# Rebalancing a scheduled attention and gated-FFN kernel: fewer operations on GpSimd, P also scaled by ScalarE

## The chip, the cores and the metric

The kernel runs on one core of one Trainium2 chip. The core has a matrix engine (TensorE, PE in the profile), three engines for elementwise work (VectorE or DVE, ScalarE or ACT, GpSimd or POOL), and SyncE (SP), which here issues nearly all transfers. Each engine runs its own list of instructions in order and waits on semaphores for the others. The metric is the device time in microseconds, the median over runs.

## The reference

Attention over q, k, v of shape (8 batches, 8 heads, 576 positions, 64), followed by a normalised gated feed-forward over the 4608 resulting rows of 512.

```python
scores = q @ k.T / 8
mask_local   = (rel >= 0) & (rel < 32)                    # heads 0..3, rel = i - j
mask_strided = (rel >= 0) & (j % 32 == i % 32)            # heads 4..7
attn = softmax(where(mask, scores, -1e9)) @ v
x  = attn.transpose(0, 2, 1, 3).reshape(4608, 512)
xn = x / sqrt(mean(x * x) + 1e-6) * rms_g
y  = (silu(xn @ w_gate) * (xn @ w_val)) @ w_out           # 512 -> 1536 -> 512
```

## The kernel before, in words

The rows of x are cut into nine chunks of 512, one per 512 columns of a matmul. The feed-forward is the dense work: weights and activations are split into a high and a low part (xh, xl, hh, hl), and three products of 128x512 matmuls stand for one in full precision. Chunks 0 to 2 go unit by unit (12 units of 128 hidden columns): L1040 makes g and v, L1053 and L1055 turn g into a gate, L1066 multiplies by v (one "gate" per unit, 36 in all), L1073 and L1082 split the product, L1092 multiplies by w_out. Chunks 3 and 4, then 5 and 6, then 7 and 8 go in pairs with a seven-product scheme (L1851 for two of the pairs, L1464 and L1630 for the last). During chunk 0 the weights are converted as they arrive (L2072 to L2094), and once during the first half transforms of the weights are made (L1144, L1148, L1230 to L1241).

The attention of later batches is woven between these dense matmuls. Its unit is a batch, two heads and up to two tiles of queries. Two units make a pair, and pairs alternate between two buffers, pp0/pT0 and pp1/pT1. A pair goes: scores on PE into one PSUM bank (L614; earlier units L715), row maxima and the masked copy out of the bank on DVE (L620), exponentials on ACT (L627), row sums and their reciprocals on DVE (L642, L643, tile my), normalising P by them on POOL (L650, tile pp, one instruction per unit), a transpose on DVE (L664), and seven block moves pp to pT that SP issues (L667). Two pairs are a group; its values are made on PE together (L836, into the same bank) and copied to raw, the rows of x, by ACT (L881) or DVE (L883). Then come squares and roots of a chunk (L916, L921, L980 to L990).

The order of all this is not written out. `Plan.op` collects operations with a cost in ns, what they read and write, and the engines that may run them. `forward` is a list scheduler: for each engine it takes the operations that can start soonest (within a "hold", one number per engine) and among them the one with the earliest due time; of an operation with two possible engines it takes an engine only if no other would finish it sooner. `port` marks operations which the plan lets run on only one of VectorE and GpSimd at a time. `series` and `latest` work out due times in rounds, with the sets PASS_A and PASS_B (holds; spacing of chains; allowance for a transfer; rounds). The resulting order of each engine is fixed in the program.

Of the kernel before, what the change touches and what calls it, by code (L numbers as in the profile page):

```python
# [14 lines left out]
AF = mybir.ActivationFunctionType  # L15
# [17 lines left out]
NX = 3  # L33
# [5 lines left out]
RES0 = [0, 7, 14, 20, 26]  # L39
NEG = -1.0e9  # L40
NCST = 512
DW = 4
VIN = 4
MSL = 8
# [50 lines left out]
MARG = 0.0  # L95
# [36 lines left out]
PVF = 1  # L132
HLO = 9
TABLE = 1283.0
PORT = True
PASS_A = ([0.0, 0.0, 150.0, 400.0], 0.4, 4000.0, 7)
PASS_B = ([25.0, 450.0, 300.0, 800.0], 0.1, 8000.0, 9)
SWITCH = 220000.0
PLAP = 140.0
LATE = -100000.0  # L140
# [21 lines left out]
class Plan:  # L162
# [18 lines left out]
    def op(self, eng, cost, at, fn, reads=(), writes=(), bytes_=0, rel=0.0, lock=(), tab=None, port=False, chain=False, also=None, early=0.0):  # L181
        i = len(self.ops)
        self.early.append(early)
        self.lift.append(0.0 if chain else self.boost)
        deps = set()
        for r in reads:
            if r in self.writer:
                deps.add(self.writer[r])
        for w in writes:
            if w in self.writer:  # L190
                deps.add(self.writer[w])
            deps.update(self.readers.get(w, ()))
        for r in reads:
            self.readers.setdefault(r, []).append(i)
        for w in writes:
            self.writer[w] = i
            self.readers[w] = []
        deps.discard(i)
        if eng == "PE":
            if self.serial:  # L200
                deps.add(self.last_pe)
            self.last_pe = i
        if also is None:
            ways = {eng: (cost, port or eng == "Pool", fn)}
        else:
            ways = {e: (c, p or e == "Pool", lambda e=e: fn(e)) for e, c, p in [(eng, cost, port)] + list(also)}
        self.ops.append((ways, deps, bytes_, rel, lock, tab, chain))
# [64 lines left out]
    def forward(self, users, due, hold, due2=None, hold2=None):  # L272
        ops, n = self.ops, len(self.ops)
        left = [len(o[1]) for o in ops]
        end, on = [0.0] * n, [None] * n
        ready = [None] * n
        free, avail = {}, {}

        def enter(i):
            ways, deps, _, rel, _, _, _ = ops[i]  # L280
            ready[i] = {e: max([end[d] + (0.0 if on[d] == e and not ops[d][2] else self.lat(i)) for d in deps] + [rel]) for e in ways}
            for e in ways:
                avail[e].append(i)
        for o in ops:
            for e in o[0]:
                free.setdefault(e, 0.0)
                avail.setdefault(e, [])
        for i in range(n):
            if not left[i]:
                enter(i)  # L290
        dma = 0.0
        held = {}
        table = "exp"
        port = (0.0, None)
        names = ("PE", "DVE", "ACT", "Pool")
        out = []

        def start(i, e):
            s = max(free[e], ready[i][e])
            for b in ops[i][4]:  # L300
                t, who = held.get(b, (0.0, e))
                s = max(s, t if who == e else t + self.LAT)
            if ops[i][0][e][1] and port[1] != e:
                s = max(s, port[0])
            return s
        while len(out) < n:
            best = None
            for e, lst in avail.items():
                cand = []
                for i in lst:  # L310
                    s = start(i, e)
                    ways = ops[i][0]
                    if len(ways) > 1:
                        f = s + ways[e][0] - MARG
                        if any(x != e and start(i, x) + ways[x][0] < f for x in ways):
                            continue
                    cand.append((s, due[i] - self.lift[i], i))
                if not cand:
                    continue
                soon = min(cand)[0] + (hold[names.index(e)] if e in names else 0.0)  # L320
                k = min((c for c in cand if c[0] <= soon), key=lambda c: (c[1], c[0], c[2]))
                if best is None or k < best[0]:
                    best = (k, e)
            (s, _, i), e = best
            ways, _, nb, _, lock, tab, _ = ops[i]
            cost, pt, fn = ways[e]
            if tab and tab != table:
                table = tab
                cost += TABLE
            done = s + cost + self.TAIL[e]  # L330
            for b in lock:
                held[b] = (done, e)
            if pt:

                port = (done - PLAP, e)
            for x in ways:
                avail[x].remove(i)
            free[e] = s + cost
            on[i] = e
            if nb:  # L340
                dma = max(dma, s) + nb / 380.0
                end[i] = dma + 2000.0
            else:
                end[i] = done
            out.append((i, e, s, end[i]))
            if due2 is not None and s > SWITCH:
                due, hold = due2, hold2
            for u in users[i]:
                left[u] -= 1
                if not left[u]:  # L350
                    enter(u)
        return out
# [3 lines left out]
def attn_moe(ctx: ExitStack, tc: tile.TileContext, qT: bass.AP, kT: bass.AP, vl: bass.AP, vs: bass.AP,  # L356
             wgv: bass.AP, wo: bass.AP, gain: bass.AP, consts: bass.AP, out: bass.AP):
    nc = tc.nc
# [68 lines left out]
    def dve(n, rate=0.96):  # L427
        return 75 + n / rate
# [4 lines left out]
    def way(name, *ways):  # L433

        return [w for w in ways] if name in ALT else []
# [162 lines left out]
    def step_e(i):  # L598
# [31 lines left out]
        def rest():  # L630
# [14 lines left out]
            for y, (m_, n_) in enumerate(((m0, n0), (m1, n1))):  # L645
                def norm(e, y=y, m_=m_, n_=n_):
                    g = slice(4 * y, 4 * y + 4, 3 - n_)
                    s = mx2[x][:m_, y].rearrange("q h t -> q (h t)") if n_ == 2 else mx2[x][:m_, y, :, 0]
                    v = PX[x][:m_, :, g]
                    (nc.vector if e == "DVE" else nc.gpsimd).tensor_tensor(  # L650
                        out=v, in0=v, in1=s.unsqueeze(1).unsqueeze(3).broadcast_to([m_, 4, 2 * n_, 32]), op=ALU.mult)
                op("Pool", 500 * n_, 0, norm, reads=[("sm", x, y)], writes=[("pu", x, y)], also=way("h", ("DVE", dve(256 * n_), True)))
        return scores, rd, 2 * nt * (0.84 * P + 2), rest

    units = []
# [268 lines left out]
    def rms(c, bk, at):  # L924
# [60 lines left out]
        for kc in range(KC):  # L985
            op("DVE", dve(CH) + 50, at + kc,
               lambda kc=kc: nc.vector.scalar_tensor_tensor(out=rt[:, kc], in0=rt[:, kc], scalar=gt[:, kc:kc + 1],
                                                            in1=roots["srt"], op0=ALU.mult, op1=ALU.mult),
               reads=["srt", "gt"], writes=[("raw", c % NX, kc)])

    def convert(c, at, kcs=range(KC)):
        rt = raw[c % NX]
# [1295 lines left out]
```

## Time and profile before

| | |
|---|---|
| runs shown | median 1011.04 us, 1009.02 to 1013.16 |
| the profiled execution: its time | 1004.59 us |
| its span, mean granted clock | 1002.4 us, 0.991 |
| PE / DVE / ACT / POOL busy | 970.6 / 739.5 / 495.9 / 311.9 us |
| DMA, mean over the span | 218 GB/s |

The numbers of the page belong to the one profiled execution, whose time lies 6.45 us below the median of the runs. A busy engine is one whose instructions run; PE's matmuls overlap, so a chain of 128x512 matmuls shows one new start every 0.227 us although one lasts about 0.4. A wait is an engine's idle time with the name of what ended it.

### The profile page before, as it was taken

What the parts mean: (1) busy time and instruction counts of PE and PEld (TensorE: products, weight loads), DVE (VectorE), ACT (ScalarE), POOL (GpSimd) and SP (SyncE); (2) the same over time, 40 slices, a digit from 0 to 9 for tenths busy, and PEclk for the clock granted to TensorE, in tenths of its full rate; (3) what the DMA queues carried; (4) which work ended last, traced back from release to release, by engine and by line L of the source; (5) the groups of instructions that cost most, each with busy time, mean ns of one, the idle gap of its engine ahead of it and who ended that gap; (6) DMA issues with size and microseconds to landing.
All of it is one profiled execution on the core that took longest, in us unless ns stands there. A gap on an engine that the chain in (4) does not pass through costs nothing.

```text
span 1002.4 us, 16255 instructions
## 1 busy us (share of the span) xinstructions
PE 970.6 (97%) x5212; PEld 778.7 (78%) x5212; DVE 739.5 (74%) x1741; ACT 495.9 (49%) x1392; POOL 311.9 (31%) x294
## 2 busy tenths in 40 slices
PE   8899999999998999999999999999999999999998
PEld 6777766778876777887888887888887787888886
DVE  5889999888977859489665648954565888456981
ACT  6999865555456434455555333534252423234530
POOL 6333346776557536135101113110002210001200
PEclk9999999999999999999999999999999999999999
DMA  9999654666656464254766698575587644793551
GB/s 312 367 389 341 222 206 150 219 223 210 221 176 233 144 232 144 63 171 149 237 211 239 213 315 304 181 269 177 171 300 278 209 167 168 238 334 120 159 168 74
DMA packets 88469, 218.13 MB, mean 218 GB/s; under 512 B 11840, under 2 KB 35392, under 8 KB 88384
## 3 DMA queue, kind: packets, MB, share of 16 engines
q1 hardware_dynamic: 87616, 216.23, 62.3%
q10 hardware_dynamic: 768, 0.85, 0.3%
q8 instruction: 42, 0.69, 0.3%
q14 instruction: 43, 0.35, 0.1%
HBM read 162.06 MB, written 47.19 MB: 209 GB/s over the span
## 4 chain that ended last, share of the span: by engine, by line
PE 78%; DVE 8%; DMA 7%; issue 3%; SPq 2%; ACT 2%; POOL 1%; ACTq 0%; DVEq 0%; POOLq 0%
PE acc L1092 18%; PE acc L1851 9%; PE g L1040 8%; PE v L1040 7%; PE g L1851 6%; PE v L1851 6%; PE v L1464 3%; PE pair L1464 3%; PE g L1464 3%; PE pair L614 3%; PE pair L836 2%; PE v L1630 2%; PE g L1630 2%; PE acc L1630 2%; SPq L667 2%
## 5 line engine op out<-in xcount | busy, mean ns | idle before, releaser
L1092 PE MATMUL acc<-or,hh 128*128 128x512 f32 x480 | 153.4, 401 | 0.6 <-POOL or L2094 0.6
L650 POOL TENSOR_TENSOR pp<-pp,my 96x512 f32<-96x512 f32 (+2 forms) x68 | 69.8, 1046 | 231.4 <-DVE my L643 48.3
L627 ACT ACTIVATE pp<-pp,my 96x128 f32<-96x128 f32 (+2 forms) x248 | 96.2, 391 | 39.7 <-DVE my L620 27.8
L1092 PEld LDWEIGHTS acc<-or,hh 128*128 128x128 f32 x480 | 90.3, 191 | 22.3 <-POOL or L2094 1.5
L1040 PE MATMUL g<-xh,wg 128*128 128x512 f32 x288 | 93.0, 404 | 3.0 <-DVE e L1055 3.0
L1092 PE MATMUL acc<-or,hl 128*128 128x512 f32 x240 | 94.7, 395 | 0.6 <-POOL hl L1082 0.6
L1040 PE MATMUL v<-xh,wv 128*128 128x512 f32 x280 | 90.0, 402 | 1.9 <-DVE e L1066 1.2
L1082 POOL TENSOR_TENSOR hl<-e,hh 128x512 fp32r<-128x512 f32 x36 | 52.4, 1455 | 82.3 <-ACT hh L1073 82.2
L620 DVE CUSTOM_DVE_ANT_0 pp<-pair,cb 96x128 f32<-96x128 f32 (+2 forms) x248 | 55.4, 282 | 18.5 <-DMA pT<-pp 8.4
L1040 PEld LDWEIGHTS g<-xh,wg 128*128 128x128 f32 x288 | 51.9, 189 | 16.4 <-DVE e L1055 3.9
L1040 PEld LDWEIGHTS v<-xh,wv 128*128 128x128 f32 x280 | 51.3, 190 | 15.7 <-DVE e L1066 2.5
L1092 PE MATMUL acc<-or,xh 128*128 128x512 f32 x192 | 59.7, 392 | 0.0
L1040 PE MATMUL g<-xl,wg 128*128 128x512 f32 x144 | 56.5, 392 | 0.0
L1040 PE MATMUL v<-xl,wv 128*128 128x512 f32 x140 | 54.8, 392 | 0.0
L1092 PEld LDWEIGHTS acc<-or,hl 128*128 128x128 f32 x240 | 45.8, 191 | 11.1 <-POOL hl L1082 1.1
L627 ACT ACTIVATION_READ_ACCUMULATOR pp<-pp,my 96x1 f32 (+2 forms) x248 | 46.7, 188 | 0.0
L881 ACT COPY raw<-pair 128x192 f32<-128x192 f32 (+12 forms) x103 | 22.9, 348 | 47.4 <-PE pair L836 43.7
L664 DVE STREAM_TRANSPOSE pp<-pp 128x1024 f32<-128x1024 f32 x34 | 42.0, 1237 | 3.2 <-POOL pp L650 3.2
L614 PEld LDWEIGHTS pair<-xx,xx 64*96 64x96 f32 (+2 forms) x496 | 29.2, 170 | 16.7 <-issue 8.5
L1092 PEld LDWEIGHTS acc<-or,xh 128*128 128x128 f32 x192 | 35.7, 188 | 8.1 <-issue 0.5
L614 PE MATMUL pair<-xx,xx 64*96 64x128 f32 (+2 forms) x496 | 36.4, 285 | 4.4 <-ACT raw L881 2.4
L921 POOL TENSOR_TENSOR ssq<-ssq,srt 128x512 f32<-128x512 f32 x21 | 28.7, 1366 | 32.7 <-ACT srt L916 32.7
(661 smaller groups left out, 2496.9 us busy)
## 6 DMA issues: line engine op xcount, KB each, us to landing
or<-wos SPq DMA_DIRECT2D x72, 512.0 KB, 4.4
wv<-wsv SPq DMA_DIRECT2D x29, 512.0 KB, 7.6
or<-tg SPq DMA_DIRECT2D x22, 512.0 KB, 5.8
th<-tg SPq DMA_DIRECT2D x21, 512.0 KB, 6.4
tl<-tg SPq DMA_DIRECT2D x21, 512.0 KB, 4.1
wg<-wsg SPq DMA_DIRECT2D x19, 512.0 KB, 8.7
xx<-in_qT_dram SPq DMA_DIRECT2D x31, 288.0 KB, 5.1
xx<-in_kT_dram SPq DMA_DIRECT2D x28, 288.0 KB, 3.0
```

What stands on the lines that cost most here:

```text
L614: nc.tensor.matmul(out=sp[h][:, t].rearrange("q x k -> q (x k)"), lhsT=qt[r, q0:q0 + m], rhs=kt[r, k0:k0 + P], start=True, stop=True)
L620: nc.vector.tensor_tensor_reduce(out=PX[x][:m, :, g0 + 2 * h + t], in0=sp[h][:, t], in1=mk[t], scale=-0.125, scalar=3.0e38, op0=ALU.add, o ...
L627: nc.scalar.activation(out=v, in_=v, func=AF.Exp, scale=-1.0, bias=mx2[x][:m, u, h, t:t + 1], accum_out=su2_[x][:m, u, h, t, 0:1])
L650: (nc.vector if e == "DVE" else nc.gpsimd).tensor_tensor(out=v, in0=v, in1=s.unsqueeze(1).unsqueeze(3).broadcast_to([m_, 4, 2 * n_, 32]), ...
L664: op("DVE", DVT + 2 * CH / 0.96, 0, lambda: nc.vector.transpose(out=pq[x], in_=pq[x]), reads=[], writes=[("pu", x, 0), ("pu", x, 1), ("pp" ...
L921: op("Pool", pool(CH), at, lambda e: (nc.vector if e == "DVE" else nc.gpsimd).tensor_tensor(out=ssq, in0=ssq, in1=roots["srt"], op=ALU.add ...
L1040: nc.tensor.matmul(out=out, lhsT=wt[:, w, sl], rhs=xhl[x, kc], start=(kc == 0 and i == 0), stop=(kc == KC - 1 and i == 2))
L1082: (nc.vector if n == "DVE" or h else nc.gpsimd).tensor_tensor(out=hl[h], in0=e, in1=hh[h].bitcast(F32), op=ALU.subtract)
L1092: nc.tensor.matmul(out=acc[t], lhsT=x[h][:, sl], rhs=wt[:, w], start=(u == 0 and i == 0), stop=(u == NU - 1 and i == 2))
L1464: nc.tensor.matmul(out=banks[bk], lhsT=w, rhs=X[a, k].tile(y), start=start and k == 0 and i == 0, stop=stop and k == 1 and i == 2, skip_gr ...
L1630: nc.tensor.matmul(out=banks[bks[j]], lhsT=tile(v, k, j), rhs=x.tile(y), start=start and k == 0 and i == 0, stop=stop and k == KT - 1 and ...
L1851: nc.tensor.matmul(out=banks[bk], lhsT=w, rhs=xtile(a, k, y), start=start and k == 0 and i == 0, stop=stop and k == 1 and i == 2, skip_gro ...
```

## The change

Five things change in the plan's rules, and one in the work.

- `POOLP = 700`: where an operation may run on several engines, GpSimd's finishing time counts as 700 ns later.
- The normalising of P for later units (L650) may run on GpSimd or ScalarE; ScalarE then issues one activation (copy with a per-row factor) per head and tile, 4 or 2 per unit. It could run on GpSimd alone before, since `way("h", ...)` is switched off.
- The final scaling of x in `rms` (L987) is marked with `port`, so that the plan keeps it off GpSimd's time. The instruction is the same.
- PE operations outside the dense chains count 80 ns less (`SMD`); among PE operations those of the kind just run are preferred by 600 ns (`KIN`); the cost of a switch of kind is a parameter, zero (`SWC`).
- Transfers are planned at 345 bytes per ns in place of 380 (`DMR`), and the holds and rounds of the two passes are other numbers.

```diff
+POOLP = 700.0
+DMR = 345.0
+SWC = 0.0
+SMD = 80.0
+KIN = 600.0
-PASS_A = ([0.0, 0.0, 150.0, 400.0], 0.4, 4000.0, 7)
-PASS_B = ([25.0, 450.0, 300.0, 800.0], 0.1, 8000.0, 9)
+PASS_A = ([0.0, 0.0, 210.0, 560.0], 0.3, 4000.0, 7)
+PASS_B = ([60.0, 466.0, 445.0, 585.0], 0.1, 4000.0, 11)
...
         if eng == "PE":
+            if not chain:
+                cost = max(cost - SMD, 150.0)
...
-                        f = s + ways[e][0] - MARG
-                        if any(x != e and start(i, x) + ways[x][0] < f for x in ways):
+                        f = s + ways[e][0] - MARG + POOLP * (e == "Pool")
+                        if any(x != e and start(i, x) + ways[x][0] + POOLP * (x == "Pool") < f for x in ways):
                             continue
-                    cand.append((s, due[i] - self.lift[i], i))
+                    cand.append((s, due[i] - self.lift[i] - (KIN if e == "PE" and ops[i][6] == kind else 0.0), i))
...
+            if e == "PE" and ops[i][6] != kind:
+                kind = not kind
+                cost += SWC
...
-                dma = max(dma, s) + nb / 380.0
+                dma = max(dma, s) + nb / DMR
...
+                    if e == "ACT":
+                        for h in range(2):
+                            for t in range(n_):
+                                w = PX[x][:m_, :, 4 * y + 2 * h + t]
+                                nc.scalar.activation(out=w, in_=w, func=AF.Copy, scale=mx2[x][:m_, y, h, t:t + 1])
+                        return
...
-                op("Pool", 500 * n_, 0, norm, reads=[("sm", x, y)], writes=[("pu", x, y)], also=way("h", ("DVE", dve(256 * n_), True)))
+                op("Pool", 500 * n_, 0, norm, reads=[("sm", x, y)], writes=[("pu", x, y)], also=[("ACT", 2 * n_ * 293, False)])
...
-               reads=["srt", "gt"], writes=[("raw", c % NX, kc)])
+               reads=["srt", "gt"], writes=[("raw", c % NX, kc)], port=PORT)
```

Every engine's order differs. Three places follow; line numbers of the change are 11 to 17 higher than those of before.

TensorE, at the end of chunk 2 (units 0 and 1 of the next weights), where the bank "pair" is passed between scores and values. Before, from a group's values on:

```order
L836 MATMUL pair<-pT_98,vt_86 64x128 x2
L836 MATMUL pair<-pT_98,vt_87 64x128 x4
L836 MATMUL pair<-pT_99,vt_87 64x128 x6
L1040 MATMUL v<-xh_676,wv_545 128x512 x2
L1040 MATMUL v<-xl_683,wv_545 128x512
L614 MATMUL pair<-xx_84,xx_83 96x128 x8
```

and in the change, from the scores ahead of the same values on:

```order
L625 MATMUL pair<-xx_84,xx_83 96x128 x4
L1057 MATMUL g<-xh_654,wg_534 128x512 x2
L1057 MATMUL g<-xl_665,wg_534 128x512
L1057 MATMUL v<-xh_654,wv_586 128x512 x2
L1057 MATMUL v<-xl_665,wv_586 128x512
L853 MATMUL pair<-pT_98,vt_86 64x128 x2
L853 MATMUL pair<-pT_98,vt_87 64x128 x4
L853 MATMUL pair<-pT_99,vt_87 64x128 x6
L625 MATMUL pair<-xx_84,xx_83 96x128 x8
```

The next scores follow the values at once (3 dense matmuls stood between), and 6 dense matmuls stand ahead of the values, where 15 did.

GpSimd in chunk 2, two consecutive pairs' P (tiles pp_96 and pp_97). Before:

```order
L650 TENSOR_TENSOR pp_96<-pp_96,my_105 126x4x128
L650 TENSOR_TENSOR pp_96<-pp_96,my_105 108x4x2x32
L1148 TENSOR_TENSOR tt<-tt 128x256
L650 TENSOR_TENSOR pp_97<-pp_97,my_106 108x4x128
L650 TENSOR_TENSOR pp_97<-pp_97,my_106 108x4x2x32
```

and ScalarE in the change, around the end of that chunk (L638 are the exponentials, L898 the copies to raw, L665 the new activations):

```order
L638 ACTIVATE pp_97,sv_107<-pp_97,my_106 96x4x32 x4
L665 ACTIVATE pp_96<-pp_96,my_105 96x4x32 x4
L898 COPY raw_78<-pair 128x6x10
L898 COPY raw_79<-pair 128x6x8
L638 ACTIVATE pp_97,sv_107<-pp_97,my_106 96x4x32 x4
L933 ACTIVATE srt<-raw_78 128x512
```

Of a pair's two units one has gone to ScalarE, between the exponentials of the other buffer.

SyncE, the last two groups of block moves. Before:

```order
L667 DMA pT_98<-pp_96 32x256 x7
L1118 DMA out_dram<-xh_7085 128x512
L1248 DMA tl_7117<-tg_150 128x1024
L1118 DMA out_dram<-xl_7093 128x512
L1248 DMA th_7126<-tg_150 128x1024
L2125 DMA or_7129<-wos_119 128x1024
L667 DMA pT_99<-pp_97 32x256 x7
```

and in the change:

```order
L684 DMA pT_98<-pp_96 32x256 x7
L1265 DMA tl_7085<-tg_150 128x1024
L1265 DMA th_7090<-tg_150 128x1024
L2142 DMA or_7093<-wos_114 128x1024
L2142 DMA or_7114<-wos_115 128x1024
L2142 DMA or_7145<-wos_116 128x1024
L2142 DMA or_7171<-wos_117 128x1024
L1135 DMA out_dram<-xh_7181 128x512
L1135 DMA out_dram<-xl_7187 128x512
L2142 DMA or_7199<-wos_118 128x1024
L684 DMA pT_99<-pp_97 32x256 x7
```

Nine transfers lie between the two groups, where five did, and the two outputs nearest the end of the queue follow the last group instead of preceding it.

More of the change, by code (lines that the diff above doesn't have):

```diff
@@ L294, in forward @@
         port = (0.0, None)
+        kind = False
         names = ("PE", "DVE", "ACT", "Pool")
```

## The prediction

> **What bounds the kernel now.** I read the head of the page first, then the busy time by stretch, then who made TensorE (PE) wait, then the chain of work.
>
> ```profile
> span 1002.4 us, 16255 instructions
> PE 970.6 (97%) x5212; PEld 778.7 (78%) x5212; DVE 739.5 (74%) x1741; ACT 495.9 (49%) x1392; POOL 311.9 (31%) x294
> PE 78%; DVE 8%; DMA 7%; issue 3%; SPq 2%; ACT 2%; POOL 1%; ACTq 0%; DVEq 0%; POOLq 0%
> ```
>
> TensorE is busy for 97% and carries 78% of the chain. The change adds and drops no matrix work, so it can only win or lose where the matmuls wait: 1002.4 - 970.6 = 31.8 us idle, some of it at the two ends, plus what a lowered clock costs. These are the longer waits between the ends (line engine, releaser: total, times, longest):
>
> ```profile
> PE pair L836 <- DMA pT<-pp: 3.7, 2, 2.3
> PE g L1040 <- DVE e L1055: 3.0, 2, 2.0
> PE pair L614 <- ACT raw L881: 2.4, 1, 2.4
> PE pair L715 <- DVE mx L732: 2.3, 1, 2.3
> PE pair L614 <- DVE my L620: 1.8, 2, 1.1
> PE pair L836 <- DVE my L620: 1.5, 1, 1.5
> PE v L1040 <- DVE e L1066: 1.2, 1, 1.2
> PE g L1851 <- DVE or L1901: 1.2, 1, 1.2
> ```
>
> They sum to 17.1 us. Nearly all belong to the attention that is woven between the dense matmuls: scores (L614, L715) wait for the one score bank to be emptied, values (L836) for the probabilities to arrive. No line names POOL, but POOL sits inside those loops. The busy time by stretch shows who is short there (columns: stretch, length, busy PE, PEld, DVE, ACT, POOL, granted clock, DMA share, GB/s):
>
> ```profile
> 100.00:150.00 50.00, 47.73 (x300) 36.00 (x298) 47.07 (x142) 36.40 (x112) 20.77 (x20) 1.00 0.61 217
> 150.00:200.00 50.00, 46.89 (x254) 35.55 (x255) 45.52 (x132) 29.18 (x91) 35.65 (x30) 0.97 0.51 184
> 300.00:350.00 50.00, 44.34 (x287) 34.57 (x286) 39.88 (x121) 30.21 (x102) 31.89 (x29) 0.97 0.58 188
> ...
> 145.00:155.00 10.00, 7.42 (x44) 5.10 (x43) 9.83 (x41) 9.18 (x27) 4.73 (x4) 0.84 0.45 154
> 295.00:310.00 15.00, 12.01 (x84) 9.36 (x85) 12.09 (x48) 10.09 (x40) 8.43 (x9) 0.89 0.72 246
> 355.00:370.00 15.00, 13.00 (x58) 10.17 (x54) 10.38 (x20) 4.48 (x10) 6.22 (x6) 0.89 0.66 210
> 795.00:805.00 10.00, 7.69 (x40) 6.07 (x40) 7.13 (x10) 3.95 (x8) 1.47 (x1) 0.83 0.75 272
> ```
>
> From 100 to 200 us VectorE is 93% busy: that stage is short of VectorE. From 300 to 350 no engine is full and PE stands 5.7 us: that stage is short of time in a loop of hand-offs. And each of the four longest waits is followed by a dip of the granted clock: 10 us at 0.83 instead of 1.00 is 1.7 us lost, and 15 us at 0.89 is 1.65 us. So a wait of two to three microseconds costs about 1.7 us more than itself.
>
> By the Trainium skill ("TensorE: Matmul & The Clock Gate", Part 1) the clock halves after at least one idle window of about 3.4 us. The rows contradict that as a floor: the longest wait listed is 2.4 us and the clock still dipped. By the rule my sum below would lose one 1.7 us term and read -5.4 us.
>
> **The change, part by part.**
>
> *P on two engines.* Normalising P is one instruction per unit on POOL; a pair of units was two in a row, ahead of the transpose. Counted in the order, 35 of 68 go to ScalarE, mostly one unit of each pair; each becomes 2 or 4 small activations (130 in all).
>
> ```profile
> 315.78 2.49 POOL pp L650 x2
> ...
> 318.30 1.25 DVE pp L664
> ...
> 330.78 2.73 PE acc L1092 x12
> ```
>
> ```profile
> L650 POOL TENSOR_TENSOR pp<-pp,my 96x512 f32<-96x512 f32 x32 | 34.5, 1097 | 83.1 <-DVE my L643 31.9 <-DMA xx<-in_kT_dram 24.6 <-DMA pT<-pp 14.2
> L627 ACT ACTIVATE pp<-pp,my 96x128 f32<-96x128 f32 x128 | 49.7, 391 | 17.1 <-DVE my L620 11.6 <-DMA tg<-tl 4.5 <-DMA vt<-in_vl_dram 1.0
> L881 ACT COPY raw<-pair 128x192 f32<-128x192 f32 x29 | 9.2, 356 | 12.8 <-PE pair L836 10.8 <-PE pair L842 2.0
> ```
>
> The new activation has no row. The nearest are the exponential over the same 128 columns with a per-row operand (0.391 us) and a plain copy of 192 (0.356). I take 0.36, nearer the copy, since the new one has a per-row factor but no exponential. Bounds: 0.28 (the copy scaled down from 192 columns, an estimate) to 0.39. Four take 1.4 us beside 1.1 us on POOL, so the pair's two steps last about 1.4 instead of 2.2 to 2.5: roughly 0.9 us less per turnaround. ScalarE gains 130 x 0.36 = 47 us and gives up 18 output copies, 18 x 0.356 = 6.4: +40 on 496, about 54% of the span. In 300 to 350 it stands at 30.2 of 50, which covers the 8 us or so it gets there; without that cover its copies out of the bank (L881) would be late, and with them the next scores.
>
> In the crunch of 295 to 330 us four pairs chase each other through two buffers, two turnarounds in series on each: 2 x 0.9 = -1.8 us. Against it, the new order is tighter there: between the scores of one pair and the following values stand 6 dense matmuls where 15 stood, and behind those values none where 3 stood (three take 0.7 us: the last row of the chain is 12 in 2.73). I charge the 0.7 for the latter, and for the former a quarter of the 2.0 us of lost cover, 0.5, since those values did not wait at all before. Shorter turnarounds also let the evacuation go to whichever of VectorE and ScalarE is free; the wait on ACT L881 (2.4) should halve, -1.2. Term: **-1.8**, bounds -7 (all waits there and the dip) to +4 (tighter order, full price).
>
> *Two late rounds.* Here the order gives more room.
>
> ```profile
> 607.44 0.88 PE L836 MATMUL pair<-pT,vt 108*64 108x128 f32 x12 [1.38 <-DMA pT<-pp]
> ...
> 800.69 1.55 PE L836 MATMUL pair<-pT,vt 128*64 128x96 f32 x16 [2.31 <-DMA pT<-pp]
> ```
>
> ```profile
> 785.27 4.31 SPq L667 DMA_DIRECT2D pT<-pp  x7
> 789.68 0.53 SPq L1118 DMA_DIRECT2D out_dram<-xh  x1
> 790.31 0.38 SPq L1248 DMA_DIRECT2D tl<-tg  x1
> 790.78 0.40 SPq L1118 DMA_DIRECT2D out_dram<-xl  x1
> 791.28 0.38 SPq L1248 DMA_DIRECT2D th<-tg  x1
> 791.75 0.45 SPq L2125 DMA_DIRECT2D or<-wos  x1
> 792.30 5.08 SPq L667 DMA_DIRECT2D pT<-pp  x7
> ```
>
> At 607 the values come 63 dense matmuls after the last scores of their group; in the new order 150. At 0.227 us each that is 20 us more room for a wait of 1.38: it goes, **-1.4** (bounds -1.4 to 0, should the or and w loads ahead on SP's queue still be late). At 800 the room grows from 75 to 84 matmuls, +2.0 us, and the half-turn above gives 0.9; and between the last two groups of seven transfers SP issued five others from 789.68 to 792.30, with 15 dense matmuls between the two scores; the new order has nine there, but 66 matmuls (15 us) to issue them in. 2.9 us covers the 2.31, so the wait goes, and with it the dip of 1.7: **-4.0** (bounds -4.0 to 0, if an output transfer in front holds SP up).
>
> *Bias away from POOL.* 71 instructions leave POOL; 35 are P, the rest go to VectorE, among them all eight weight subtractions L2094; with them come 18 output copies L883.
>
> ```profile
> L2094 DVE TENSOR_TENSOR or<-th,or x8: 678/681/1779, 49.4 to 130.1; 128x512 fp32r<-128x512 f32 x8
> L2094 POOL TENSOR_TENSOR or<-th,or x4: 1260/1278/1751, 58.0 to 175.6; 128x512 fp32r<-128x512 f32 x4
> ...
> L883 DVE COPY raw<-pair x38: 200/326/557, 20.5 to 771.5; 128x192 f32<-128x192 f32 x6, 128x84 f32<-128x84 f32 x3, 128x120 f32<-128x120 f32 x3, 128x96 f32<-128x96 f32 x3
> ...
> 156.51 1.90 DVE L2087 SCALAR_TENSOR_TENSOR th<-or 128x512 uint32<-128x512 uint32 x1
> 156.59 1.27 POOL L1144 TENSOR_TENSOR tt<-wg 128x512 f32<-128x512 f32 x1
> ```
>
> (The first three rows give min/median/max ns.) Between the 9th and the 13th gate of the first two chunks, in the stage short of VectorE, six L2094 (6 x 0.68 = 4.1 us) and four copies (4 x 0.33 = 1.3) are new: +5.4 us. The last two rows show the return: a VectorE step took 1.90 us while POOL ran 1.27 beside it, against the 0.68 of a like 512-column step, so one such meeting costs VectorE 1.2 us. Six POOL steps gone, perhaps a quarter of them such meetings, give back 1.8. Net +3.6, of which PE sees what its slack does not take (VectorE is idle 7.4 of those 100 us): **+2.5**, bounds -1.8 (the relief larger than the work) to +5.4. Elsewhere VectorE has idle time to hold the added steps.
>
> *Other constants* (transfer rate, cheaper attention on PE, preference for one kind of work, holds) only move order. Transitions between attention and dense rows go from 185 to 187, so nothing is saved by grouping. For the waits on L1055 (2.0 at 360, with its dip of 1.65) and L1901 (1.2), whose causes are steps moved about by the new order, I take half of 4.85: **-2.4**, bounds -4.9 to +3 (they form again one hand-off later). *SBUF-only scaling of x* enters the planner's port rule alone; no instruction changes, zero.
>
> Sum: -1.8 - 1.4 - 4.0 + 2.5 - 2.4 = **-7.1 us** on the profiled execution (1002.4 span, 1004.59 its time). The runs shown have a median of 1011.04, 6.5 above that; the sum carries over: **1004**.
>
> **Rivals.**
> (a) *VectorE becomes the bound.* Place: 100 to 200 us. If POOL was not what slowed it, the 5.4 us land on an engine 93% busy, with its tighter rounds at 300 (+4) and re-formed waits at 360 (+3). It decides once the added steps exceed the 7.4 us of idle time. Late rounds still win: 5.4 + 4 + 3 - 5.4 = +7: 1018. For it: L732, L1055, L1066, L620 are all VectorE releasers. Against: POOL's longer steps are what it meets.
> (b) *The room is eaten elsewhere*: ScalarE's four activations stand in its in-order queue before copies and exponentials, and a late round finds another transfer in front. Then only -1.4 and half of -4 hold, against +2.5: about -1: 1010.
> (c) *Relief larger than the work*: with POOL emptied, VectorE steps as at 156.51 shrink to 0.68, and the waits from 145 to 370 (all listed but the first and the last, 12.2 us) with their three dips (5.0) go by half: -8.6, with the late rounds' -5.4 and no +2.5: -14, 997. By the Trainium skill ("SBUF — State Buffer", Who interferes with whom) VectorE and GpSimd share one port pair as an exclusive lock; the 156.51 row agrees.
>
> **How the numbers follow.** Forecast 0.47, (a) 0.19, (b) 0.22, (c) 0.12. Its own range is 998 to 1009. 8 in 10, with the bounds above and parts of (a) and (c): 994 to 1017. Half a percent, 5 us, is about what a measurement of this kernel tells from none. Faster by more: 0.40 of the forecast, all of (c), 0.04 of (b): 0.56. Same: 0.07, 0.16 of (b), 0.02 of (a): 0.25. Slower: 0.17 and 0.02: 0.19.
>
> **What would show it.** Right: no wait of PE L836 on pT transfers and no clock dip near 800; DVE at L664 starting within 1.6 us of the reciprocals; POOL near 235 us busy, ACT near 535. Wrong: DVE over 96% from 100 to 200 with PE under 46 of 50 there; new waits of scores on ACT copies near 300; new activations far from 0.36 us; a new dip of the clock anywhere.

## The result, and the profile after

| | before | change |
|---|---|---|
| median of the runs (6 each, same chip) | 1010.03 us (1006.52 to 1015.48) | 1002.05 us (998.86 to 1003.35) |
| ratio, 95% interval | | 0.9918 [0.9895, 0.9942] |
| profiled execution: its time, span, clock | 1004.59, 1002.4 us, 0.991 | 1002.72, 1000.7 us, 0.987 |

The change is faster by 0.8%, some 8 us; the forecast was 1004, inside a range of 994 to 1017. The two profiled executions differ by 1.9 us only, because the one of before was unusually fast. A second profile of before (first experiment) had a span of 1008.5 us, and both are used here.

The page of the change, busy times and the chain by engine, and two groups of its instructions, P on GpSimd and P on ScalarE:

```profile
span 1000.7 us, 16323 instructions
...
PE 970.4 (97%) x5212; PEld 778.9 (78%) x5212; DVE 738.7 (74%) x1796; ACT 532.9 (53%) x1503; POOL 224.9 (22%) x223
...
PE 84%; DVE 7%; DMA 4%; ACT 2%; SPq 1%; issue 1%; POOL 0%; DVEq 0%; ACTq 0%
...
L667 POOL TENSOR_TENSOR pp<-pp,my 96x512 f32<-96x512 f32 (+3 forms) x33 | 32.1, 979 | 231.6 <-DMA wv<-wsv 62.7
...
L665 ACT ACTIVATE pp<-pp,my 96x128 f32<-96x128 f32 (+2 forms) x130 | 41.5, 393 | 14.6 <-DVE my L654 14.3
```

GpSimd went from 311.9 to 224.9 us and ScalarE from 495.9 to 532.9. VectorE executes 55 instructions more and is busy no longer. What TensorE waits for now:

```profile
PE pair L625 <- ACT raw L898: 5.3, 1, 5.3
PE pair L853 <- DVE my L631: 4.4, 4, 2.3
PE acc L1109 <- DVE or L2111: 3.6, 2, 2.4
PE acc L732 <- DMA xx<-in_kT_dram: 3.2, 1, 3.2
PE v L1057 <- DVE wv L2111: 1.7, 2, 1.1
```

The values' waits on the block moves (before: two, 3.7 us together) are gone. A longer wait is new: scores L625, 5.3 us, from 308 us on. The waits on L2111 (L2094 of before, 0.7 and 0.6 us there) are longer too. By stretch (columns as before, the eighth is the granted clock):

```profile
100.00:150.00 50.00, 48.78 (x283) 36.78 (x283) 47.34 (x141) 39.74 (x107) 18.73 (x17) 1.00 0.67 232
150.00:200.00 50.00, 44.41 (x237) 33.06 (x236) 44.92 (x136) 29.97 (x94) 21.16 (x19) 0.93 0.45 152
300.00:350.00 50.00, 40.62 (x255) 31.61 (x253) 37.18 (x114) 33.74 (x118) 24.35 (x22) 0.90 0.61 198
355.00:370.00 15.00, 15.00 (x85) 12.23 (x84) 13.43 (x27) 6.25 (x15) 6.03 (x5) 1.00 0.58 191
795.00:805.00 10.00, 10.00 (x69) 7.80 (x68) 8.97 (x15) 5.46 (x11) 0.00 (x0) 1.00 0.81 265
```

At 300 to 350 PE stands 9.4 us where it stood 5.7, and the clock is lower. From 150 to 200 it stands 5.6 us where it stood 3.1, again at a lower clock. At 360 and at 800 nothing is lost any more.

**Where the time is.** All kernels here execute the same 3656 matmuls of 512 columns. Taking 0.2268 us for each of them from the length of a stretch leaves the time that dense work does not explain: attention on PE, waits, a lowered clock. The stretches end at instructions on VectorE that every kernel has: the 13th, 25th and 33rd multiplication by v (L1066, in the change L1083), the 9th and the 13th L1901 (in the change L1918; about 520 and 645 us), and the end. This table is worked out from the starts of the matmuls and the ends of those instructions, from one profile each:

| us not explained by dense work | to 13th | to 25th | to 33rd (~395) | to ~520 | to ~645 | to the end | early, late sum |
|---|---|---|---|---|---|---|---|
| before | 74.7 | 28.5 | 19.1 | 13.9 | 15.2 | 21.9 | 122.3, 51.0 |
| before, second profile | 76.6 | 28.2 | 21.7 | 13.4 | 16.9 | 22.4 | 126.5, 52.7 |
| the change | 79.0 | 33.6 | 15.2 | 14.0 | 12.3 | 17.4 | 127.8, 43.7 |

Against the second profile of before the change wins 9 us behind 395 us and loses 1.3 ahead of it; against the first, 7.3 and 5.5.

### The profile page after: what moved, and what is told of

Same layout as the page of the kernel before. It is cut to its first block, busy times and chain, and to the rows that moved or that the text cites. A ratio compares the mean times of both kernels' runs of the same rounds, so it can differ in the third digit from the quotient of the medians.

```text
span 1000.7 us, 16323 instructions
## 1 busy us (share of the span) xinstructions
PE 970.4 (97%) x5212; PEld 778.9 (78%) x5212; DVE 738.7 (74%) x1796; ACT 532.9 (53%) x1503; POOL 224.9 (22%) x223
## 4 chain that ended last, share of the span: by engine, by line
PE 84%; DVE 7%; DMA 4%; ACT 2%; SPq 1%; issue 1%; POOL 0%; DVEq 0%; ACTq 0%
PE acc L1109 21%; PE acc L1868 10%; PE g L1057 8%; PE v L1057 7%; PE g L1868 7%; PE v L1868 6%; PE pair L1481 3%; PE g L1481 3%; PE v L1481 3%; PE pair L625 3%; PE pair L853 2%; PE v L1647 2%; PE g L1647 2%; PE acc L1647 2%; PE acc L1481 2%; SPq L684 1%
## 5 line engine op out<-in xcount | busy, mean ns | idle before, releaser
L638 ACT ACTIVATE pp<-pp,my 96x128 f32<-96x128 f32 (+2 forms) x248 | 96.2, 391 | 34.7 <-DVE my L631 33.5
L1109 PEld LDWEIGHTS acc<-or,hh 128*128 128x128 f32 x480 | 90.1, 190 | 27.1 <-DVE or L2111 4.5
L667 POOL TENSOR_TENSOR pp<-pp,my 96x512 f32<-96x512 f32 (+3 forms) x33 | 32.1, 979 | 231.6 <-DMA wv<-wsv 62.7
L1099 POOL TENSOR_TENSOR hl<-e,hh 128x512 fp32r<-128x512 f32 x36 | 49.6, 1378 | 112.2 <-ACT hh L1090 105.5
L631 DVE CUSTOM_DVE_ANT_0 pp<-pair,cb 96x128 f32<-96x128 f32 (+2 forms) x248 | 55.6, 283 | 14.3 <-DMA pT<-pp 8.2
L665 ACT ACTIVATE pp<-pp,my 96x128 f32<-96x128 f32 (+2 forms) x130 | 41.5, 393 | 14.6 <-DVE my L654 14.3
L638 ACT ACTIVATION_READ_ACCUMULATOR pp<-pp,my 96x1 f32 (+2 forms) x248 | 46.8, 189 | 0.0
L681 DVE STREAM_TRANSPOSE pp<-pp 128x1024 f32<-128x1024 f32 x34 | 42.1, 1237 | 4.1 <-ACT pp L665 1.8
L625 PEld LDWEIGHTS pair<-xx,xx 64*96 64x96 f32 (+2 forms) x496 | 29.4, 171 | 17.2 <-issue 9.5
L625 PE MATMUL pair<-xx,xx 64*96 64x128 f32 (+2 forms) x496 | 36.6, 286 | 5.3 <-ACT raw L898 5.3
```

Source lines behind the costliest of these rows:

```text
L625: nc.tensor.matmul(out=sp[h][:, t].rearrange("q x k -> q (x k)"), lhsT=qt[r, q0:q0 + m], rhs=kt[r, k0:k0 + P], start=True, stop=True)
L631: nc.vector.tensor_tensor_reduce(out=PX[x][:m, :, g0 + 2 * h + t], in0=sp[h][:, t], in1=mk[t], scale=-0.125, scalar=3.0e38, op0=ALU.add, o ...
L638: nc.scalar.activation(out=v, in_=v, func=AF.Exp, scale=-1.0, bias=mx2[x][:m, u, h, t:t + 1], accum_out=su2_[x][:m, u, h, t, 0:1])
L665: nc.scalar.activation(out=w, in_=w, func=AF.Copy, scale=mx2[x][:m_, y, h, t:t + 1])
L667: (nc.vector if e == "DVE" else nc.gpsimd).tensor_tensor(out=v, in0=v, in1=s.unsqueeze(1).unsqueeze(3).broadcast_to([m_, 4, 2 * n_, 32]), ...
L681: op("DVE", DVT + 2 * CH / 0.96, 0, lambda: nc.vector.transpose(out=pq[x], in_=pq[x]), reads=[], writes=[("pu", x, 0), ("pu", x, 1), ("pp" ...
```

## The experiments

The expectations name these theories. **A**: the shorter turnaround of P. **B**: the gain is all in the new numbers and their order, and the engines do not matter. **C**: relief of VectorE from an emptier GpSimd. **A2**: the planner needs the extra choice of engines, or the emptier GpSimd, to form the better order and its room for the late rounds, even if they are worth nothing on the chip. "Order kept" means that each engine's list stands as planned and only the named instructions change engine; "planned again" means that the planner ran with the edit. Every ratio is against runs of before on the same chip.

**1. before_again**: the kernel before, unchanged.

> The kernel before once more, unchanged. Every theory: ratio 1.000 within 0.003. Its profile tells how far two executions of one kernel differ: the first profiled execution was 6.5 us below the median of its runs. If that lies in the granted clock, this span comes with a lower mean clock than 0.991 and more half-clock windows; if it lies in waits, the waits of PE differ from those shown.

Measured 0.9997 [0.9974, 1.0021], 1010.82 us. Its waits and two of its stretches:

```profile
PE g L1040 <- DVE e L1055: 5.4, 3, 2.1
PE pair L836 <- DMA pT<-pp: 4.0, 2, 2.2
PE pair L614 <- ACT raw L881: 2.4, 1, 2.4
PE pair L715 <- DMA xx<-in_kT_dram: 2.4, 1, 2.4
```

```profile
800.00:815.00 15.00, 12.76 (x74) 10.22 (x69) 12.54 (x18) 5.14 (x11) 1.48 (x1) 1.00 0.77 265
605.00:620.00 15.00, 13.19 (x68) 10.40 (x67) 9.57 (x16) 6.45 (x14) 4.24 (x3) 0.89 0.84 297
```

The waits are those of the first profile, but the dip of the clock behind the last round (here at 808 us) is not there, and one stands behind the round at 610. So a wait of 2 us may or may not bring a dip.

**2 and 3. P alone: p_act_in_before and p_pool_in_after**, order kept. In before, the second unit of each pair normalises on ScalarE; in the change, every unit goes back to GpSimd.

```diff
 # p_act_in_before
+                    if y == 1:
+                        for h in range(2):
+                            for t in range(n_):
+                                w = PX[x][:m_, :, 4 * y + 2 * h + t]
+                                nc.scalar.activation(out=w, in_=w, func=AF.Copy, scale=mx2[x][:m_, y, h, t:t + 1])
+                        return
 # p_pool_in_after
-                    if e == "ACT":
-                        for h in range(2):
...
-                        return
```

> The kernel before, every engine's order kept, except that the second unit's P of each pair is scaled by ScalarE at the place where POOL had it. Theory A (shorter turnaround of the pairs, as predicted: 0.9 us each, two in series in the crunch, a little in the last round): -2 to -4 us, ratio 0.996 to 0.998, the wait of PE L836 on pT near 800 about 1 us shorter. Theory B (the gain of the change is all in the new order): ratio 1.000 within 0.002. Theory C (POOL steps that hold VectorE up): -3 to -5 us with VectorE busy 5 us lower.

> The changed kernel, order kept, except that the units' P that ScalarE scaled is scaled by POOL at the same place. Theory A: 2 to 4 us of the 8 us gain go, ratio to the kernel before 0.994 to 0.997. Theory B: still 0.992. Theory C: VectorE busy rises by 5 us and the ratio to 0.996.

Measured 1.0023 [1.0004, 1.0042] and 0.9904 [0.9874, 0.9934]. Given to before, the second engine costs a little; taken from the change, it costs nothing. Theory A falls: in before's order the wait of the values near 800 is 2.4 us with the second engine, no shorter than without. In the trace of p_pool_in_after the wait at 308 us stays as it is in the change:

```profile
PE pair L626 <- ACT raw L893: 5.0, 1, 5.0
```

**4. sub_pool_in_after**: the change, order kept, with the eight weight subtractions L2111 (L2094 of before) back on GpSimd.

```diff
-        op("Pool", pool(512), at, lambda e: (nc.vector if e == "DVE" else nc.gpsimd).tensor_tensor(
+        op("Pool", pool(512), at, lambda e: (nc.vector if key not in (("g", 0), ("o", 1, 0), ("g", 8), ("v", 10), ("o", 4, 0), ("g", 11), ("o", 5, 0), ("o", 6, 0)) else nc.gpsimd).tensor_tensor(
```

> The changed kernel, order kept, except that the eight weight subtractions which POOL did before are given back to POOL at the same place. Theory A (they load a VectorE that is 93% busy from 100 to 200 us): faster by 1 to 3 us than the changed kernel, ratio 0.989 to 0.991. Theory C (POOL steps hold VectorE up as long as they save it): the same as the changed kernel or 2 us slower, 0.992 to 0.994.

Measured 0.9914 [0.989, 0.9939]: no difference from the change that can be told; the interval still holds the 0.989 to 0.991 of theory A. Its VectorE is as busy as with the eight steps on it, and TensorE's longest waits on the weight subtractions stay, though these eight are back on GpSimd:

```profile
PE 966.6 (97%) x5212; PEld 776.2 (78%) x5212; DVE 739.1 (74%) x1788; ACT 532.5 (53%) x1503; POOL 234.5 (24%) x231
...
PE acc L1110 <- DVE or L2112: 3.6, 2, 2.4
```

The time that dense work does not explain in these three, in the columns of the table above:

| | to 13th | to 25th | to 33rd | to ~520 | to ~645 | to the end | early, late |
|---|---|---|---|---|---|---|---|
| p_act_in_before | 76.8 | 29.3 | 21.2 | 14.0 | 15.2 | 22.9 | 127.3, 52.1 |
| p_pool_in_after | 80.0 | 34.9 | 12.5 | 15.0 | 12.3 | 16.9 | 127.4, 44.2 |
| sub_pool_in_after | 75.7 | 34.7 | 15.0 | 14.0 | 12.3 | 16.3 | 125.4, 42.6 |

Each goes with the order it has, whichever engine does the moved work.

**5 to 8. Parts of the change, planned again.** numbers_only keeps the constants and the `port` mark, without bias and without ScalarE; edits_old_numbers keeps bias and ScalarE, with the old constants and no mark; after_no_act and after_no_bias each take one edit from the change.

```diff
 # numbers_only: both; after_no_bias: the first; after_no_act: the second
-POOLP = 700.0
+POOLP = 0.0
...
-... writes=[("pu", x, y)], also=[("ACT", 2 * n_ * 293, False)])
+... writes=[("pu", x, y)], also=[])
 # edits_old_numbers
-DMR = 345.0
+DMR = 380.0
-SMD = 80.0
-KIN = 600.0
+SMD = 0.0
+KIN = 0.0
-PASS_A = ([0.0, 0.0, 210.0, 560.0], 0.3, 4000.0, 7)
-PASS_B = ([60.0, 466.0, 445.0, 585.0], 0.1, 4000.0, 11)
+PASS_A = ([0.0, 0.0, 150.0, 400.0], 0.4, 4000.0, 7)
+PASS_B = ([25.0, 450.0, 300.0, 800.0], 0.1, 8000.0, 9)
...
-               reads=["srt", "gt"], writes=[("raw", c % NX, kc)], port=PORT)
+               reads=["srt", "gt"], writes=[("raw", c % NX, kc)])
```

> Planned afresh with the new numbers (transfer rate, attention cost, preference of kind, holds, rounds) and the port mark, but without the bias away from POOL and with P on POOL alone. Theory B (the new numbers make the better order, the engines do not matter): ratio to the kernel before 0.990 to 0.994. Theory A2 (the planner needs the emptier POOL to find the room for the late rounds): 0.998 to 1.004, with PE L836 waiting on pT again.

> Planned afresh with the bias of 700 and P allowed on ScalarE, but with the old numbers and without the port mark. Theory B: 0.998 to 1.006. Theory A2: 0.992 to 0.996, the late waits on pT gone.

> The change without ScalarE for P, planned afresh. Theory B: 0.990 to 0.994, since moving P back in the fixed order cost nothing. Theory A2: 0.996 to 1.000, since the planner then books 2 us of POOL in a row per pair.

> The change without the bias (POOLP 0), planned afresh. Theory B: 0.990 to 0.994. Theory A2: 0.994 to 0.998, VectorE busy higher by its meetings with POOL.

| | ratio, 95% | to 13th | to 25th | to 33rd | to ~520 | to ~645 | to the end | early, late |
|---|---|---|---|---|---|---|---|---|
| numbers_only | 1.0004 [0.998, 1.0027] | 82.7 | 26.1 | 28.6 | 16.5 | 11.3 | 15.3 | 137.4, 43.1 |
| after_no_act | 0.999 [0.9968, 1.0012] | 79.7 | 27.1 | 30.3 | 16.5 | 11.2 | 15.6 | 137.1, 43.3 |
| after_no_bias | 1.0036 [1.0017, 1.0055] | 83.3 | 31.7 | 22.0 | 14.5 | 12.5 | 17.0 | 137.0, 44.0 |
| edits_old_numbers | 0.993 [0.9904, 0.9957] | 80.9 | 35.1 | 14.5 | 12.0 | 14.8 | 17.9 | 130.5, 44.7 |

All four have the late gain, whatever was left out, so no single edit is its cause. numbers_only and edits_old_numbers share no edit at all, and both have it; whether any other new plan would have it too, no run shows. Without the bias, without ScalarE or without both, the early part costs 9 to 10 us more than the change's, and the gain is used up. With both and the old constants (edits_old_numbers) the result cannot be told from the change. The waits of numbers_only show it: these are five of the larger ones between 100 and 400 us.

```profile
PE pair L859 <- DVE pT L814: 5.2, 1, 5.2
PE pair L853 <- DVE my L631: 4.2, 2, 2.1
PE pair L732 <- DVE mx L749: 2.8, 1, 2.8
PE g L966 <- DVE xx L962: 2.6, 1, 2.6
...
PE g L1057 <- ACT srt L997: 2.2, 2, 1.4
```

Behind 400 us the whole list of numbers_only is one wait, and none on the block moves, with GpSimd as busy (317.9 us) as in before:

```profile
PE g L1868 <- DVE or L1918: 1.2, 1, 1.2
```

So the edits matter, but through the plan: without the bias or the choice of ScalarE a worse early order comes out, while moving the same P on the chip under one order changes nothing (2, 3). B (numbers alone) falls with its total. A2 has three of the four ratios, but not its place: it had numbers_only wait for pT again in the late rounds, and the room there comes without either edit; what the edits buy is the early part. after_no_bias, at 1.0036, is slower than any theory had it. The `port` mark was not tried by itself.

**9 to 11. Halves of the two orders.** Both plans are made in one program; the operations that one plan starts before a time T stand in its order and on its engines, all the rest in the other's. T is the planner's own time.

```diff
+        one, two = old, new          # new_then_old_400: new, old
+        out = [t for t in one if t[2] < 400000.0]   # old_then_new_650: 640000.0
+        had = set(t[0] for t in out)
+        out += [t for t in two if t[0] not in had]
+        return [fresh[i][0][e][2] for i, e, _, _ in out]
```

> One kernel out of both plans: every operation that the plan of before starts in its first 400 us stands in the order (and on the engine) of before, all others in the order of the change. Theory 'the gain sits in the late part of the new order' (in the profiles so far every new plan ends its part from gate 32 to the end 5 to 8 us sooner than before, 609 down to about 602 to 604 us, and the early part costs or gains by itself): early part as before (392 to 396 us to gate 32), late part as in the change (about 603): ratio 0.990 to 0.995, so the change's gain with the early edits left out. Rival 'early and late belong together' (the late gain is only what an early loss pushed back, and the seam costs a wait): 0.997 to 1.001, with the late part back at 608 us or more.

> The reverse: the operations that the changed plan starts in its first 400 us in its order and on its engines (so with the bias and P on ScalarE there), all others in the order of before. Theory 'late part': early part as in the change (394 to 397 us to gate 32), late part as before (607 to 611): ratio 0.999 to 1.003. Rival 'the gain is made early (turnarounds, emptied GpSimd)': 0.992 to 0.996. 'Both halves carry some': in between.

> Order of before for what its plan starts in the first 640 us, the order of the change behind that: only the last round of attention (the group near 800 us, a wait of 2.3 us and a clock dip of 1.7 in the first profile) and the end of the program are new. Prediction's term for that round: -4.0; the end was 1.3 shorter in every new plan: ratio 0.994 to 0.996. If the round at 607 us and the order ahead of it carry the late gain: 0.998 to 1.000.

| | ratio, 95% | to 13th | to 25th | to 33rd | to ~520 | to ~645 | to the end | early, late |
|---|---|---|---|---|---|---|---|---|
| old_then_new_400 | 0.99 [0.9873, 0.9928] | 81.2 | 28.7 | 21.6 | 14.1 | 12.3 | 17.0 | 131.5, 43.4 |
| new_then_old_400 | 0.9986 [0.9965, 1.0007] | 78.4 | 34.2 | 14.7 | 13.5 | 15.0 | 24.0 | 127.3, 52.5 |
| old_then_new_650 | 1.0016 [0.9992, 1.0039] | 80.9 | 28.8 | 20.1 | 13.9 | 17.0 | 24.1 | 129.8, 55.0 |

The whole gain lies behind 400 us: with the old order (and its choice of engines) ahead of it and the new one behind, all of it is there; the other way round, none that can be told from nothing. Behind 400 us PE is busy for 598.6 of 600 us in old_then_new_400, and waits once:

```profile
400.00:1000.00 600.00, 598.56 (x2986) 488.55 (x2984) 406.02 (x864) 255.69 (x654) 67.22 (x59) 1.00 0.60 205
```

```profile
PE acc L1130 <- DMA or<-wos: 1.4, 1, 1.4
```

In new_then_old_400 it is 593.3, with the waits of before:

```profile
400.00:1000.00 600.00, 593.25 (x2946) 483.20 (x2945) 406.30 (x841) 237.57 (x601) 95.24 (x82) 0.99 0.60 204
```

```profile
PE pair L874 <- DMA pT<-pp: 4.0, 2, 2.7
PE pair L1502 <- ACT pT L1515: 1.3, 1, 1.3
PE g L1889 <- DVE or L1939: 1.2, 1, 1.2
```

With a median of 1000.23 us old_then_new_400 cannot be told from the change; the intervals overlap.

old_then_new_650 was meant to price the last round alone. It has no wait of the values there either, but its seam made a new one of its own, so the price stays open:

```profile
PE acc L1889 <- ACT tt L1907: 5.1, 1, 5.1
```

**12. late_values_in_before**: before's order, the values behind a planned time of 590 us placed 3 us later, with whatever depends on them.

```diff
+            at[i] = max([s + 3000.0 * (s > 590000.0 and e == "PE" and self.old[i][0][e][2].__name__ == "values")]
+                        + [at[d] + 1e-3 for d in self.old[i][1]])
```

> Before's order with one thing moved: the values of the rounds behind 590 us (six places on TensorE) stand 6 to 12 dense matmuls (1.4 to 2.7 us) later, everything else as it was. This is the prediction's mechanism of the late rounds alone. If it is right, no wait of values on pT transfers near 607 and 800 us and no half-clock window behind them: -1.4 to -2.2 and -2.3 to -4.0, together -3.7 to -6: ratio 0.994 to 0.9965. Rival 'the wait moves on' (the copies, the next scores or the final rows are then late by the same amount, or the dip comes elsewhere): 0.998 to 1.001.

Measured 0.9986 [0.9965, 1.0007], 1009.73 us. The plan's times are earlier than the chip's, and the round at 607 us was planned before 590: its values did not move, and still wait (2.6 us). Those from 725 us on moved by 6 to 12 matmuls. PE's waits from 760 to 820 us:

```profile
PE acc L1130 <- DMA or<-wos: 1.4, 1, 1.4
PE acc L1130 <- DVE hh L2019: 1.4, 1, 1.4
PE pair L646 <- DVE raw L921: 1.0, 1, 1.0
```

The wait on pT near 800 (2.2 us in before) is gone. In its place the next scores wait for the copies of the values ahead of them (1.0), since the values moved right up to them in the same bank, and a product waits for hh (1.4). The wait moved on, and no change of the time can be told; the time that dense work does not explain, behind the 33rd multiplication, is 55.6 us in its profile, more than in either profile of before. The interval does not exclude the 2.3 us that the expectation gave the round at 800 at least. More room behind the values' inputs was not enough here, where the values then crowd what follows. In the change it was made at the other end: the last two groups of scores stand behind 2650 and 2716 dense matmuls where they stood behind 2710 and 2725, and the values behind 2778 and 2802 as before (at 607 us: scores 1854 for 1956, values 2006 for 2021; counted in the traces).

## Why the prediction was right, and where it was not

The forecast of -7.1 us stands against some -8 us, by its terms as follows. The measured column compares means of the tables' columns. Early part: six profiles with before's order (before twice, p_act_in_before, old_then_new_400 and _650, late_values_in_before), four with the change's (the change, p_pool_in_after, sub_pool_in_after, new_then_old_400). Late part: four of each (before twice, p_act_in_before, new_then_old_400; the change, p_pool_in_after, sub_pool_in_after, old_then_new_400).

| term | predicted | measured |
|---|---|---|
| late rounds | -5.4 | -8.6 (51.0 to 52.7, mean 52.1; with the change's order 42.6 to 44.2, mean 43.5) |
| VectorE in 100 to 200 us | +2.5 | +0.2 (to the 13th: 78.1 and 78.3) |
| P, and the crunch at 300 | -1.8 | to the 25th: 28.6 and 34.4, +5.7 |
| other constants, 360 us | -2.4 | to the 33rd: 20.3 and 14.4, -6.0 |

The stretches overlap a little with the terms' places, and profiles of one order differ by up to 6.5 us to the 13th, so the +0.2 there is good to a few us only; the last two rows belong together, -4.2 predicted and -0.3 measured. The sum of the column is -8.7.

**Late rounds: right, and larger.** No wait of values on pT near 607 and 800, and no dip behind them, as forecast. Behind 400 us this is the whole list of before's second profile, then of the change:

```profile
PE pair L836 <- DMA pT<-pp: 4.0, 2, 2.2
PE pair L1464 <- ACT pT L1477: 1.3, 1, 1.3
PE g L1851 <- DVE or L1901: 1.2, 1, 1.2
PE acc L1092 <- DMA or<-wos: 1.2, 1, 1.2
PE acc L1092 <- ACT raw L881: 0.6, 1, 0.6
```

```profile
PE acc L1109 <- DMA or<-wos: 1.2, 1, 1.2
PE acc L1109 <- ACT pp L638: 0.3, 1, 0.3
```

8.3 us of waits became 1.5. Beside the two rounds' 4.0 went the wait of L1464, which is in no term, and that of L1851, of which half stood under the other constants. Over the four profiles of each kind the listed waits shrink by 5.8 us. Dips of the clock add 2.1: by the traces' clock each of the four with before's late order has one, beginning in or right behind one of the two waits (at 800.4, 612.3, 807.0 and 805.0 us; 3.4 us at half the clock, 6.8 in new_then_old_400), and the four with the change's late order have none between 400 us and the last 10 us.

One part of the reasoning does not hold: the 1.7 us for the dip at 800 was charged as if that wait always brought it. The second profile of before has the wait without that dip, and the dip behind the other round. Over the whole span the change's clock is even lower, 0.987 against 0.991 and 0.990: its early dips are longer, 6.8 us at 166 and 10.2 at 309, where before has 3.4 us near 153 and 307.

By column, the stretch with the round at 607 went from 15.6 to 12.3 and the one with the round at 800 and L1464 from 22.8 to 16.9; the one ahead of them (13.7 and 14.3) won nothing, though L1851's wait lay in it. That a shorter turnaround of P gave part of the room falls with theory A: with P on GpSimd the change's order keeps its late gain (44.2). By the counts under 12 the room came from scores that stand earlier (there the room grows from 65 to 152 and from 77 to 86 matmuls; the prediction's counts are two lower each, its differences the same). No run moves these scores alone, so that step is read off the order and not shown. Nor does a run give one round without the other, since old_then_new_650 met a wait of its own.

**P on two engines: wrong.** The step that failed is "roughly 0.9 us less per turnaround". The new activation has 0.393 us, at the upper bound of 0.39 and not the 0.36 taken; four follow each other in 1.27 us, a little under the 1.4 forecast. But in ScalarE's queue they stand behind other exponentials. Over the 34 pairs the transpose starts on average 3.29 us after its reciprocal (3.90 before, 3.64 with the change's order and P on GpSimd; worked out from the rows of L654 and L681), so some 2 us of it is no work on P at all, and of the 0.61 us won the second engine gave 0.35. In before's order it won nothing (3.97). Only 6 of 34 began within 1.6 us. The longest wait of the crunch has another source. Values and the next scores stand back to back in the new order, and the bank between them has to be emptied by ScalarE; the trace of the change at 308 us:

```profile
307.05 1.53 PE L853 MATMUL pair<-pT,vt 108*64 108x128 f32 x24 [2.26 <-DVE my L631]
...
307.96 0.39 ACT L638 ACTIVATE pp<-pp,my 96x128 f32<-96x128 f32 x1
...
308.34 1.27 ACT L665 ACTIVATE pp<-pp,my 96x128 f32<-96x128 f32 x4
309.51 0.33 ACT L898 COPY raw<-pair 128x60 f32<-128x60 f32 x2
...
312.99 0.63 ACT L933 ACTIVATE srt<-raw 128x512 f32<-128x512 f32 x1 [1.64 <-DMA out_dram<-srt]
313.52 0.33 ACT L898 COPY raw<-pair 128x60 f32<-128x60 f32 x2
...
313.90 2.02 PE L625 MATMUL pair<-xx,xx 64*96 64x128 f32 x16 [5.32 <-ACT raw L898]
```

The last two copies stand behind four more exponentials (until 311.35) and a square (L933) that then waits 1.64 us for a transfer to release its buffer. I had charged 0.7 us for the missing three matmuls and halved this very wait; it is 5.3 us. It was on the list of what would show the forecast wrong ("new waits of scores on ACT copies near 300"), and rival (b) named ScalarE's queue. It was not the four activations, though, since the wait is nearly as long with P on GpSimd (5.0), where the square waits 2.23 us.

**360 us: right in direction, larger.** PE has 15.00 of 15 us there and the full clock: all of the wait on L1055 and its dip went, where half was taken. With part of the crunch now ahead of the 25th multiplication, that stretch and the next are even together, so the early part as a whole neither wins nor loses.

**VectorE in 100 to 200: charged, and no such loss shown.** VectorE is no busier there (92.3 us of 100 after, 92.6 before), although 55 more instructions are on it. Summing for all its instructions that ran beside one of GpSimd how much longer they took than the fastest tenth of their kind (same operation and shapes), some 61 us were lost to such meetings in before and 35 in the change, 12.0 and 5.5 of them from 100 to 200 us. The relief that rival (c) named is real and about as large as the added work, where I credited 1.8 of 5.4. It brought no time: (c) placed its gain between 145 and 370 us, and the new order's first 400 us by themselves (new_then_old_400) bring none. Rival (a) did not come in its size: PE has 93.2 of those 100 us, 94.6 and 95.5 in the two profiles of before. The waits on L2111 there (1.2, 1.1 and 2.4 us) take the place of those on L732 and L1066 (2.3 and 1.2 in before).

**What made the total right.** Errors that cancel: -3.2 more in the late rounds and the +2.5 that did not come, against 3.9 of the early gain that did not come. That the total came within 1 us is in part luck; that the late rounds were the largest term, and carry the whole result, is not. Of the signs of being wrong two came: the new wait of scores on ScalarE's copies, and dips of the clock that before does not have in that length (6.8 us at 29 and 166, 10.2 at 309). PE also fell under 46 of 50 us from 150 to 200 (44.4), but without the full VectorE that the sign asked for (90%).

## What to carry to other kernels

A second engine for an operation may be worth nothing where it runs and still decide the result, because the planner makes another order with it: hold the order and move the operation, then plan again without it, and the two effects come apart. Price a list scheduler's new order stretch by stretch, with the dense work taken out; here four profiles of one late order agree within 2 us on the late part, while two spans of one kernel differ by 6. Moving a waiting step later, up against what follows it, only handed the wait on here.

## What was not expected of the hardware

One program's profiled executions had spans of 1002.4 and 1008.5 us. Most waits are the same; those on L1055 sum to 3.0 in one and 5.4 in the other, the wait on the first inputs is longer, and the clock dips elsewhere. A dip to half the clock lasts 3.4 us, or a few times that (6.8 us at 29 and 166, 10.2 us at 309 in the change, 17.1 us at 30 in old_then_new_400; read from the traces' clock). It followed waits of 2.0 to 2.4 us in one profile and not the same waits in the next. By the Trainium skill ("TensorE: Matmul & The Clock Gate", Part 1) such a drop comes after at least one idle window of about 3.4 us, and the position of the window is free-running. The lengths of 3.4 us and the changing places agree with the window; that it needs 3.4 us without matmuls does not, since no wait of before was longer than 2.4 us.
